# A spectral mixing and gated feed-forward kernel: the first two x tiles loaded in other pieces and from two queues

## The chip, the cores and the metric

The kernel runs on one core of one Trainium2 chip. The metric is the device time of one execution in microseconds (us). A core has a matrix engine (PE; PEld is its weight load, which runs beside the matmuls), a vector engine (DVE), a scalar engine (ACT), a general engine (POOL) and a sync engine (SP). Data moves between the main memory (DRAM) and the on-chip memory through 16 DMA engines. A transfer is issued by an instruction on some engine's queue: here nearly all by SP, 36 by ACT, and in later parts of the program some by POOL. SPq and ACTq in the profile are those issuing instructions.

## The reference

With x of 2048 rows and 512 columns, the reference normalizes each row, mixes it by two Fourier matrices and multiplies the result with a gate that comes from a two-layer network:

```
xn = _layernorm(x, axis=-1)
a = jnp.einsum("bsd,ed->bse", xn, dft_hid_re)
b = jnp.einsum("bsd,ed->bse", xn, dft_hid_im)
s = jnp.einsum("ts,bse->bte", dft_seq_re, a) - jnp.einsum("ts,bse->bte", dft_seq_im, b)
h = jnp.einsum("bsd,df->bsf", xn, w1) + b1
h = where(h > 0, h, 0) ** 2
g = _silu(jnp.einsum("bsf,fd->bsd", h, w2) + b2)
return x + s * g
```

The sequence matrices are 2048 x 2048, the hidden ones 512 x 512, w1 is 512 x 1792 and w2 1792 x 512. All are float32.

## The kernel before

Each float32 operand of a product is split into a high part, rounded by ACT (`split_hi`, line 134), and the rest, made by DVE (`split_lo`, line 137), and a product is three passes: high by high, high by low, low by high. The sequence product comes first. Its columns are cut into eight chunks of 256 (c = 0 to 7), and the sum over the 2048 rows into eight steps (j = 0 to 7). Step j takes the x tile j, 256 rows of x in two groups of 128 (h = 0 and 1: rows 128 j and 1024 + 128 j), one row on each of the 128 partitions, so that a tile has 128 x 2 x 512 numbers (512 KB), and the tile `u` of the sequence matrices for chunk c and step j (512 KB as well). Chunks 0 and 1 are plain products (`one_product`, line 377); chunks 2 to 7 use seven products in place of eight (`mm`, line 362). The hidden transform and the first layer (line 755) and the second layer (line 861) follow, and the output rows are finished beside the last.

The program is written in the order in which each engine runs it; no scheduler reorders it. In chunk 0 the normalization of the x tiles runs beside the products. For each step j:

- the transfers of x tile j (`load_x`, line 200) and of `u` (`load_c`, line 273), on SP's queue
- mean and variance of each row. For tile 0 DVE does it for both groups (`ln_stats`, lines 204 and 205). From tile 1 on, DVE does it for h = 0 and ACT for h = 1: the mean (`ln_mean`, line 209) and the variance (`ln_var`, lines 214 and 144)
- the root on ACT (`ln_root`, line 221), the reciprocal and a correction step on DVE (`ln_rstd`, lines 226 to 230)
- the normalized tile `xn` on DVE (`ln_xn`, line 237), its high part `xc` on ACT (line 134), its low part on DVE (line 137), and the split of `u` into `g` in the same two lines
- 24 matmuls of 512 columns (line 377), which read `xc` and `g`

Ahead of these, PE runs 14 matmuls on zeros (line 483), which no result uses. Each engine runs its instructions in order. On DVE the instructions of the first steps stand like this: statistics of tile 0, group 0; statistics of tile 0, group 1; the reciprocal for group 0; its `xn`; the low part of `g`; the reciprocal for group 1; its `xn`; a low part; statistics of tile 1, group 0; two low parts; the reciprocal for tile 1. On ACT: a table load and a root of a constant (line 465), the two roots of tile 0, the high parts of `g` and `xc` in turn, then mean and variance of tile 1, group 1, and the root of tile 1.

The transfers stand ahead of all this, and all go to SP's queue:

```
    nc.scalar.activation(stats[:, 1, 0, 0:1], eps, AF.Sqrt)
    for hs in (one, two):
        load_x(0, hs)
    for hs in (one, two):
        load_c(0, 0, hs)
    for j in range(1, 3):
        load_x(j)
        load_c(0, j)
    load_x(3)
```

`one` is the group h = 0 and `two` the group h = 1, or the first and the second half of a `u` tile. So tile 0 comes in two transfers of 256 KB, `u` of step 0 in two of 256 KB, and what follows in transfers of 512 KB.

Of the kernel before, what the change touches and what calls it, by code (L numbers as in the profile page):

```python
# [13 lines left out]
P = 128  # L14
# [114 lines left out]
def fnet_gated_kernel(ctx, tc, x, xt, ct, wd, w1, w2, b1, b2, out):  # L129
    nc = tc.nc  # L130
# [24 lines left out]
    rows = dram.tile([2 * NS, P], F32, name="rows")  # L155
# [12 lines left out]
    def buf(tag, shape, name, dtype=F32):  # L168
        return pool.tile(shape, dtype, tag=tag, bufs=3 if tag == "u" else 1, name=name)
# [24 lines left out]
    xr, xn32 = {}, {}  # L194

    def load_x(j, hs=slice(0, 2)):

        if j not in xr:
            xr[j] = buf(X_ROOM[j], [P, 2, D], f"x{j}")
        nc.sync.dma_start(xr[j][:, hs], x.rearrange("(h j p) d -> j p h d", h=2, p=P)[j][:, hs])  # L200

    def ln_stats(j, h=0):
        bn = small[:, j % 3, 6 * h:6 * h + 6]
# [65 lines left out]
    def load_c(c, j, hs=slice(0, 2)):  # L269
        if (c, j) not in raw:  # L270
            raw[c, j] = buf("u", [P, 8, CW], f"u{c}_{j}")
        q = slice(2 * hs.start, 2 * hs.stop)
        nc.sync.dma_start(raw[c, j][:, q], ct[c, j, :, q])
# [107 lines left out]
    one, two = slice(0, 1), slice(1, 2)  # L381
# [80 lines left out]
    makers["y"] = y_early  # L462
    makers["p"] = load_wd

    nc.scalar.activation(stats[:, 1, 0, 0:1], eps, AF.Sqrt)
    for hs in (one, two):
        load_x(0, hs)
    for hs in (one, two):
        load_c(0, 0, hs)
    for j in range(1, 3):  # L470
        load_x(j)
        load_c(0, j)
    load_x(3)

    warm = bank("b30", "warm")
# [120 lines left out]
    for n, s in enumerate(steps):  # L596
        c, j = s
# [445 lines left out]
    for n in range(NTC * NP):  # L1043
        c, p = divmod(n, NP)
# [110 lines left out]
def _launch(arrays, out_shape):  # L1155
    import numpy as np
    import concourse.bacc as bacc
    from concourse.bass_utils import run_bass_kernel_spmd

    nc = bacc.Bacc("TRN2", target_bir_lowering=False, num_devices=1, dynamic_dma_scratch_size=1024)  # L1160
    feed, args = {}, []
    for name, v in arrays.items():
        v = np.ascontiguousarray(v)
        feed[f"in_{name}"] = v
        args.append(nc.dram_tensor(f"in_{name}", v.shape, mybir.dt.from_np(v.dtype), kind="ExternalInput").ap())
    args.append(nc.dram_tensor("out_0", out_shape, F32, kind="ExternalOutput").ap())
    with tile.TileContext(nc, schedule_with_timeline_sim=True) as tc:
        fnet_gated_kernel(tc, *args)
    r = run_bass_kernel_spmd(nc, [feed], core_ids=[0])
    return r.results[0]["out_0"]  # L1170
# [25 lines left out]
```

## Time and profile before

| what | value |
|---|---|
| three runs | 673.10, 673.64, 673.92 us; median 673.64 |
| the profiled execution's own time | 673.52 us |
| its span, from the first instruction to the last | 671.7 us |
| granted clock of PE | 0.999 |
| busy: PE, DVE, ACT | 665.4, 597.3, 379.0 us |
| moved by DMA | 150.82 MB, 225 GB/s on average |

The profiled execution took 1.8 us more than its span, before the first instruction and after the last one. Times in the views count from the start of the span. In the view in order of time a row gives start, duration, engine, line, operation, what is written and read, how many instructions stand in the row, and in brackets how long the engine was idle before it and what ended that. A row of the chain of waits gives start, duration and what took it, followed back from the last instruction. A row of the stretches gives the stretch, its length, the busy time of PE, PEld, DVE, ACT and POOL with the number of their instructions, PE's granted clock, the share of the DMA engines and GB/s. A row on transfers gives what is moved, the engine that issues it, how many, KB of each, and us from issue to landing. q1 is SP's DMA queue and q10 ACT's; a row on a queue gives its packets, MB and its share of the 16 engines.

### The profile page before, as it was taken

To read this page: it belongs to the slowest core of one execution; us is meant where nothing else is said; L and a number is where in the kernel's file an instruction comes from. 1 tells how busy PE (TensorE), PEld (TensorE's weight loads), DVE (VectorE), ACT (ScalarE), POOL (GpSimd) and SP (SyncE) were. 2 spreads that over 40 slices of the span, in tenths; PEclk is the share of its full clock that TensorE was granted. 3 is DMA by queue.
4 is the path that set the end of the run, shared out by engine and by line. 5 is a ranking of instruction groups with operands and counts; after the bars stand their busy time and mean duration, and the time that the engine had idled before them with its cause. 6 is when DMAs were issued, how large, how long until landed. Compare 5 with 4: busy or idle time off the path is not lost.

```text
span 671.7 us, 13186 instructions
## 1 busy us (share of the span) xinstructions
PE 665.4 (99%) x5438; PEld 646.5 (96%) x5438; DVE 597.3 (89%) x833; ACT 379.0 (56%) x524; POOL 8.8 (1%) x11
## 2 busy tenths in 40 slices
PE   8999999999999999999999999999999999999997
PEld 5888889999999999999999999999999999999997
DVE  7997888999999999799899989877887889999997
ACT  6856554534445454444365547788778765454451
POOL 0000000000000000000000000000000000101011
PEclk9999999999999999999999999999999999999999
DMA  8635768646556774759688557665755866777765
GB/s 306 212 100 218 255 232 277 214 148 213 211 168 225 248 286 162 261 164 344 200 296 279 194 188 297 222 246 209 267 183 198 326 241 212 181 230 176 232 205 156
DMA packets 51739, 150.82 MB, mean 225 GB/s; under 512 B 4960, under 2 KB 19552, under 8 KB 50272
## 3 DMA queue, kind: packets, MB, share of 16 engines
q1 hardware_dynamic: 43568, 129.28, 57.1%
q10 hardware_dynamic: 6208, 18.88, 7.1%
q0 software_dynamic: 1904, 1.84, 1.9%
q8 instruction: 42, 0.69, 0.4%
q14 instruction: 17, 0.14, 0.1%
HBM read 101.98 MB, written 47.99 MB: 223 GB/s over the span
## 4 chain that ended last, share of the span: by engine, by line
PE 94%; DVE 2%; DMA 2%; ACT 1%; issue 0%; SPq 0%; DVEq 0%; ACTq 0%
PE m L362 32%; PE m_o L861 15%; PE r_B L755 13%; PE r_A L755 9%; PE pq_b L377 8%; PE r_C L755 4%; PE r_D L755 4%; PE m_last L861 4%; PE pq_ba L377 2%; PE pq_bc L377 1%; PE pq_bb L377 1%; DMA u<-in_ct 1%; DMA x<-in_x 1%; DVE g L137 1%; DVE z L1111 0%; DVE z L911 0%
## 5 line engine op out<-in xcount | busy, mean ns | idle before, releaser
L362 PEld LDWEIGHTS m<-g,xc 128*128 128x128 f32 x2016 | 229.1, 188 | 0.3 <-DVE g L137 0.2
L362 PE MATMUL m<-g,xc 128*128 128x256 f32 x2016 | 229.3, 276 | 0.1
L134 ACT ACTIVATE g<-u 128x1792 fp32r<-128x1792 f32 (+2 forms) x65 | 99.0, 1523 | 132.1 <-PE m L362 92.6
L137 DVE TENSOR_TENSOR g<-u,g 128x1792 fp32r<-128x1792 f32 (+2 forms) x65 | 116.8, 1797 | 19.3 <-ACT g L134 18.8
L861 PE MATMUL m_o<-w,g 128*128 128x256 f32 x882 | 100.5, 276 | 0.0
L861 PEld LDWEIGHTS m_o<-w,g 128*128 128x128 f32 x882 | 100.3, 188 | 0.0
L134 ACT ACTIVATE g<-hr 128x1792 fp32r<-128x1792 f32 (+2 forms) x31 | 48.2, 1566 | 39.9 <-DVE hr L296 17.7
L755 PE MATMUL r_B<-xT,w 128*128 128x256 f32 x504 | 66.5, 276 | 0.0
L377 PE MATMUL pq_b<-g,xc 128*128 128x512 f32 x240 | 65.2, 391 | 1.0 <-ACT xc L134 1.0
L755 PEld LDWEIGHTS r_B<-xT,w 128*128 128x128 f32 x504 | 61.4, 188 | 0.0
L137 DVE TENSOR_TENSOR g<-hr,g 128x1792 fp32r<-128x1792 f32 (+2 forms) x31 | 56.7, 1838 | 3.0 <-ACT g L134 2.8
L377 PEld LDWEIGHTS pq_b<-g,xc 128*128 128x128 f32 x240 | 44.8, 188 | 11.3 <-ACT xc L134 1.9
L755 PE MATMUL r_A<-xT,w 128*128 128x256 f32 x336 | 42.8, 276 | 0.0
L755 PEld LDWEIGHTS r_A<-xT,w 128*128 128x128 f32 x336 | 40.2, 188 | 0.0
L755 PE MATMUL r_B<-wdp,yg 128*128 128x256 f32 x288 | 35.9, 277 | 0.0
L284 DVE TENSOR_TENSOR u<-u 128x512 f32<-128x512 f32 x48 | 32.9, 685 | 3.0 <-DMA u<-in_ct 3.0
L755 PEld LDWEIGHTS r_B<-wdp,yg 128*128 128x128 f32 x288 | 34.1, 188 | 0.1
L861 PE MATMUL m_last<-w,g 128*128 128x256 f32 x294 | 33.5, 276 | 0.0
L861 PEld LDWEIGHTS m_last<-w,g 128*128 128x128 f32 x294 | 33.4, 188 | 0.0
L137 DVE TENSOR_TENSOR yg<-yraw,yg 128x1792 fp32r<-128x1792 f32 x13 | 26.2, 2018 | 0.7 <-ACT yg L134 0.7
L134 ACT ACTIVATE yg<-yraw 128x1792 fp32r<-128x1792 f32 x13 | 22.2, 1707 | 5.4 <-DVE yraw L293 4.4
L755 PE MATMUL r_D<-xT,w 128*128 128x256 f32 x168 | 23.6, 276 | 0.0
(187 smaller groups left out, 876.8 us busy)
## 6 DMA issues: line engine op xcount, KB each, us to landing
u<-in_ct SPq DMA_DIRECT2D x63, 512.0 KB, 3.9
hd<-h ACTq DMA_DIRECT2D x28, 512.0 KB, 4.0
hr<-hd SPq DMA_DIRECT2D x28, 512.0 KB, 3.7
wdp<-wdd SPq DMA_DIRECT2D x8, 896.0 KB, 7.2
yraw<-pqd SPq DMA_DIRECT2D x13, 512.0 KB, 6.0
pqd<-c SPq DMA_DIRECT2D x6, 1024.0 KB, 6.2
w<-w1d SPq DMA_DIRECT2D x6, 896.0 KB, 8.2
y<-y ACTq DMA_DIRECT2D x8, 512.0 KB, 5.5
```

The costliest lines, as they stand in the source:

```text
L134: nc.scalar.activation(hi, src, AF.Copy)
L137: nc.vector.tensor_tensor(lo, src, hi.bitcast(F32), op=ALU.subtract)
L284: nc.vector.tensor_tensor(t[:, 0:2], r[:, 0:1].to_broadcast([P, 2, 256]), r[:, 1:3], op=ALU.add)
L362: nc.tensor.matmul(ps[:, d], w[:, a_, d * P:(d + 1) * P], halves(mv(b_)), start=first and d == 0 and (a_, b_) == (HI, HI), stop=last and ( ...
L377: nc.tensor.matmul(accs[c][k], w, part[c, j][:, b_, 2 * h:2 * h + 2], start=j == 0 and h == 0 and (a_, b_) == (HI, HI), stop=j == NJ - 1 a ...
L755: nc.tensor.matmul(self.region(REGION[k]), w, mv, start=i == 0 and k in (1, 7), stop=i == len(ops) - 1, skip_group_check=True)
L861: nc.tensor.matmul(m[:, i * 256:(i + 1) * 256], ready[n][:, a_, H_SLOT[a], i * P:(i + 1) * P], W2[p][:, b_, b], start=p == 0 and i == 0 an ...
```

## The change

```diff
-        nc.sync.dma_start(xr[j][:, hs], x.rearrange("(h j p) d -> j p h d", h=2, p=P)[j][:, hs])
+        src = x.rearrange("(h j p) d -> j p h d", h=2, p=P)[j]
+        if j == 0 and hs == one:
+            for q, rows in ((nc.sync, slice(0, P // 2)), (nc.scalar, slice(P // 2, P))):
+                q.dma_start(xr[j][rows, hs], src[rows, hs])
+        elif j == 0:
+            nc.scalar.dma_start(xr[j][:, hs], src[:, hs])
+        else:
+            nc.sync.dma_start(xr[j][:, hs], src[:, hs])
...
+    for hs in (one, two):
+        load_x(0, hs)
     nc.scalar.activation(stats[:, 1, 0, 0:1], eps, AF.Sqrt)
     for hs in (one, two):
-        load_x(0, hs)
-    for hs in (one, two):
         load_c(0, 0, hs)
-    for j in range(1, 3):
-        load_x(j)
-        load_c(0, j)
+    for hs in (two, one):
+        load_x(1, hs)
+    load_c(0, 1)
+    load_x(2)
+    load_c(0, 2)
     load_x(3)
```

Group 0 of tile 0 is loaded by two transfers of 64 partitions (128 KB each), the first from SP's queue and the second from ACT's. Group 1 of tile 0 follows whole on ACT's queue. Both ACT transfers stand ahead of ACT's table load. Tile 1 comes in two transfers of 256 KB on SP's queue, group 1 first. The number of transfers goes from 9 to 11 over these first lines; the bytes stay the same. The instructions of PE and DVE keep their number and order.

These are the first rows of SP's queue before. x_135, x_141, x_145 and x_149 are the x tiles 0 to 3, and u_0, u_1 and u_2 the `u` tiles of steps 0 to 2; x2 stands for two such instructions.

```order
L200 DMA x_135<-in_x 128x512 x2
L273 DMA u_0_138<-in_ct 128x512 x2
L200 DMA x_141<-in_x 128x2x512
L273 DMA u_1_143<-in_ct 128x1024
L200 DMA x_145<-in_x 128x2x512
L273 DMA u_2_147<-in_ct 128x1024
L200 DMA x_149<-in_x 128x2x512
```

And the first rows of SP's queue now, where x_134, x_142, x_147 and x_151 are the x tiles 0 to 3:

```order
L203 DMA x_134<-in_x 64x512
L280 DMA u_0_139<-in_ct 128x512 x2
L207 DMA x_142<-in_x 128x512 x2
L280 DMA u_1_145<-in_ct 128x1024
L207 DMA x_147<-in_x 128x2x512
L280 DMA u_2_149<-in_ct 128x1024
L207 DMA x_151<-in_x 128x2x512
```

One transfer is gone from ahead of the two `u` transfers of step 0, and tile 1 has two places where it had one, so that what follows it has as many transfers ahead of it on SP as before.

These are the first rows of ACT before:

```order
L465 ACT_TABLE_LOAD
L465 ACTIVATE stats<-eps 128x1
L221 ACTIVATE small<-stats,eps 128x1 x2
L134 ACTIVATE g_0_176<-u_0_138 128x512
L134 ACTIVATE xc_121<-xn_0_182 128x2x256
```

And now:

```order
L203 DMA x_134<-in_x 64x512
L205 DMA x_134<-in_x 128x512
L474 ACT_TABLE_LOAD
L474 ACTIVATE stats<-eps 128x1
L228 ACTIVATE small<-stats,eps 128x1 x2
L134 ACTIVATE g_0_178<-u_0_139 128x512
L134 ACTIVATE xc_121<-xn_0_184 128x2x256
```

Two transfers, the other half of tile 0's first group and all of its second group, are now ahead of the table load.

## The prediction

> **What bounds the kernel now.** I read the page first, then the stretches, PE in order of time, the chain of waits, and at last DVE, ACT and the transfers of the first 14 us.
>
> The page's busy times, and four stretches:
>
> ```profile
> PE 665.4 (99%) x5438; PEld 646.5 (96%) x5438; DVE 597.3 (89%) x833; ACT 379.0 (56%) x524; POOL 8.8 (1%) x11
> ...
> 7.13:13.12 5.99, 5.79 (x25) 4.42 (x25) 5.51 (x16) 4.55 (x11) 0.00 (x0) 1.00 1.02 390
> 13.12:285.00 271.88, 271.88 (x2036) 257.53 (x2037) 243.69 (x335) 140.52 (x165) 0.00 (x0) 1.00 0.62 216
> 285.00:287.00 2.00, 1.95 (x16) 1.75 (x16) 2.00 (x4) 1.85 (x2) 0.00 (x0) 1.00 0.10 16
> 287.00:667.00 380.00, 380.00 (x3348) 379.87 (x3347) 339.94 (x462) 228.31 (x341) 8.65 (x7) 1.00 0.69 229
> ```
>
> PE is busy without a gap from 13.12 to 667 us, except for 0.05 us near 286. So the end moves with the moment at which PE starts step 1 of chunk 0 (13.12), one for one; the change touches only transfers ahead of that. PE's rows up to there:
>
> ```profile
> 1.22 5.10 PE L483 MATMUL warm<-idle 128*128 128x512 bf16 x14 [1.22 <-DVE idle L479]
> 7.13 0.73 PE L377 MATMUL pq_b<-g,xc 128*128 128x512 f32 x2 [0.81 <-ACT xc L134]
> ...
> 12.53 0.39 PE L377 MATMUL pq_bc<-g,xc 128*128 128x512 f32 x1
> 13.12 0.73 PE L377 MATMUL pq_b<-g,xc 128*128 128x512 f32 x2 [0.20 <-ACT xc L134]
> ```
>
> Matmuls of step 0 start 0.23 us apart, so step 1 could have started at 12.53 + 0.23 = 12.76. It starts 0.36 later, because `xc` of tile 1 is late. The chain of waits says why, by its own account:
>
> ```profile
> 0.74 0.39 SPq L200
> ...
> 1.19 0.42 SPq L200
> ...
> 1.65 0.42 SPq L273
> ...
> 2.12 0.43 SPq L273
> 2.59 5.90 DMA x<-in_x
> 8.52 0.72 ACT junk L209 x2
> ...
> 10.73 0.31 ACT small L221
> 11.85 0.56 DVE xn L237
> ...
> 13.12 0.73 PE pq_b L377 x2
> ```
>
> The reader is to see four issues on SP, then tile 1 under way for 5.90 us until 8.49, then ACT's mean, variance and root, DVE's `xn`, PE. It looks as if all that tile 1 gains were gained at the end. DVE's rows say otherwise:
>
> ```profile
> 3.43 0.69 DVE L204 BATCH_NORM_STATS2 small<-x 128x6 f32<-128x512 f32 x1 [1.72 <-DMA x<-in_x]
> 4.23 0.18 DVE L205 BATCH_NORM_AGGREGATE stats<-small 128x2 f32<-128x6 f32 x1
> 4.33 0.66 DVE L204 BATCH_NORM_STATS2 small<-x 128x6 f32<-128x512 f32 x1
> ...
> 5.12 0.13 DVE L226 RECIPROCAL small<-small 128x1 f32<-128x1 f32 x1
> ...
> 8.77 0.69 DVE L204 BATCH_NORM_STATS2 small<-x 128x6 f32<-128x512 f32 x1
> ...
> 10.18 0.68 DVE L137 TENSOR_TENSOR xc<-xn,xc 128x512 fp32r<-128x512 f32 x1
> 11.06 0.17 DVE L226 RECIPROCAL small<-small 128x2 f32<-128x2 f32 x1 [0.20 <-ACT small L221]
> ```
>
> From 3.43, when group 0 of tile 0 has landed, DVE is occupied up to tile 1's reciprocal at 11.06, and waits there for only 0.20 us. There are thus two chains of nearly equal length: tile 1 through ACT, and tile 0 through DVE, 0.20 us shorter. Tile 0's chain also sets PE's first start (7.13).
>
> **The change part by part.** The rows for the transfers, in the order of issue on SP (0.74, 1.19, 1.65, 2.12, 2.59), with the time to landing last, and ACT's rows:
>
> ```profile
> x<-in_x SPq DMA_DIRECT2D x1, 256.0 KB, 2.7
> x<-in_x SPq DMA_DIRECT2D x1, 256.0 KB, 2.9
> u<-in_ct SPq DMA_DIRECT2D x1, 256.0 KB, 3.9
> u<-in_ct SPq DMA_DIRECT2D x1, 256.0 KB, 4.6
> x<-in_x SPq DMA_DIRECT2D x1, 512.0 KB, 5.9
> ```
>
> ```profile
> 0.73 1.28 ACT L465 ACT_TABLE_LOAD   x1 [0.73 <-PEq L1160]
> ...
> 4.45 0.29 ACT L221 ACTIVATE small<-stats,eps 128x1 f32<-128x1 f32 x1 [2.22 <-DVE stats L205]
> ...
> 6.98 0.61 ACT L134 ACTIVATE g<-u 128x512 fp32r<-128x512 f32 x1
> 8.52 0.60 ACT L209 ACTIVATE junk<-x 128x512 f32<-128x512 f32 x1 [0.92 <-DMA x<-in_x]
> ```
>
> So the landings are 3.4 and 4.1 (tile 0), 5.5 and 6.7 (`u` of step 0) and 8.5 (tile 1).
>
> *Two issues ahead of ACT's table load.* At 0.4 us each, as SP's, they put the load at about 1.6 and its end at 2.9. ACT's next work is at 4.45, after 2.22 us of idleness. Cost 0; the cover is gone only if the load took over 1 us longer.
>
> *Tile 1 in two, group 1 first.* SP has one issue less ahead, so group 1 is issued at about 2.12 and has 1.25 MB up to its end in place of 1.5. Between the landings at 6.7 and 8.5, half the way is 7.6; that is when ACT comes to line 209 anyway (8.52 - 0.92 = 7.60). ACT's 0.92 us of waiting goes, but DVE, late next, needs 11.06 - 0.20 for its own work: the term is -0.20. Group 0 of tile 1 is issued at 2.6 as before, lands by 8.5, and DVE asks for it at 8.77. Cost 0, with 0.27 of cover. What follows tile 1 is issued no later than before.
>
> *Group 0 of tile 0 from two queues.* Landing 3.4 is bounded by no change from above, and from below by half the 0.70 us that lie between the two landings of tile 0, thus 3.05. It would start DVE up to 0.35 earlier. The Trainium skill, "DMA: Bandwidth & Descriptors", section "Rules for kernel authors", says not to bother with two transfers to disjoint partition halves, because both use the same 16 engines. By that rule the landing stays at 3.4; the trace before has no such pair, so it can't say. I take 3.4, since the same 256 KB have to pass, and keep 3.05 as an end; it counts only if group 1 keeps pace.
>
> *Group 1 of tile 0 on ACT's queue.* This is the term that decides. DVE does the statistics of group 1 (4.33) ahead of the reciprocal for group 0 (5.12), and all the rest is behind them. Group 1 landed at 4.1, so it had 0.2 us to spare. It is issued at about 1.19 as before, but until now nothing else was issued then: the first half of `u` came 0.46 later, behind it. Now SP issues `u` at the same moment, and both share the engines. Two rows on sharing, for 413 to 416 us, where both queues had work:
>
> ```profile
> q1 hardware_dynamic: 124, 0.80, 68.2%
> q10 hardware_dynamic: 95, 0.39, 31.5%
> ```
>
> Packets go about one for one. Then group 1 ends when about three times 256 KB have passed in place of two. At the 0.70 us that 256 KB took between tile 0's landings this is 4.1 + 0.70 = 4.8; at the pace of `u`, whose first half landed third at 5.5, it is 5.5 (upper end). The lower end is 4.1 - 0.35 = 3.75, if both queues fill the engines sooner and group 1 stays ahead. I take 4.8, the pace of the same rows of x. DVE's second statistics then start at 4.83 in place of 4.33: +0.50, for PE's first start (7.6) and for all that DVE does up to tile 1.
>
> **Sum:** +0.50 - 0.20 = +0.3 us: step 1 starts at 13.4, after a first start at 7.6, so PE's wait between the steps shrinks to 0.16. From there PE is full as before. Ends: landing at 5.5 gives 5.53 - 4.33 - 0.20 = +1.0; 3.75 with 3.05 gives -0.35 - 0.20 = -0.55. Against the profiled execution's own 673.52 the sum is 673.8, and against the median, 0.12 above that, 673.9.
>
> **The rivals.** 0.2% of this time, 1.35 us, is about what a measurement of this kernel can tell from no change; three runs lay between 673.1 and 673.9.
>
> *A: group 1 keeps its place.* ACT's issue is at the engines before SP's `u`, and lands at 4.1 or sooner. Then only -0.20 is left, with up to 0.35 more: 673.1 to 673.4. For it: ACT starts at 0.73, SP at 0.74, and the second issues come out even. Against it: packets of two queues alternate.
>
> *B: slower, ACT's transfer waits behind SP's.* The rows for a transfer of ACT in the middle of the kernel, and for SP's packets between 409 and 412.9:
>
> ```profile
> 408.99 0.34 ACTq L845 DMA_DIRECT2D hd<-h  x1
> ...
> hd<-h ACTq DMA_DIRECT2D x1, 512.0 KB, 9.5
> ...
> q1 hardware_dynamic: 276, 1.33, 95.9%
> ```
>
> The whole of 409 to 412.9 belongs to q1: ACT's transfer moved nothing for 4 us, and landed after 9.5. If group 1 waits like that behind both halves of `u`, it lands no sooner than 6.7: 6.73 - 4.33 - 0.20 = +2.2, 675.8; behind tile 1 too, at 8.5, +4.0, 677.6. It decides from a landing of 5.9 on (5.88 - 4.33 - 0.20 = 1.35). Against it: at 409 SP's queue had megabytes waiting, while at 1.19 each queue has one transfer under way. The page "DMA: Bandwidth & Descriptors" of the Trainium skill, section "Queues, rings and completion order", has each engine go round the queues packet by packet; by that rule B can't happen and 4.8 stands. The rows at 413 agree, those at 409 don't, so B keeps a chance.
>
> *C: a remainder.* Another placement of transfers, or a first transfer on ACT's queue that starts slowly, shifts a later wait such as the one near 286. No row prices it.
>
> **How the numbers follow.** Forecast (-0.1 to +1.0): 0.53. A: 0.25. B: 0.14. C: 0.08, half to each side. Within 0.2% lie nearly all of the forecast and of A: 0.50 + 0.23 = 0.73. Slower are B, 0.03 of the forecast and half of C: 0.20. Faster is the rest, 0.07. The forecast's own range is 673.5 to 674.7. The range takes A's -0.55 and the forecast's +1.0 with 0.4 us for the scatter of the runs, and the nearest part of B: 672.7 to 675.4. It leaves out most of B and C.
>
> **What would show it.** Right: DVE's second statistics start near 4.8 and wait there for a DMA; PE's first real matmul is near 7.6 and step 1 near 13.4; ACT has no wait ahead of the mean of tile 1; the 0.20 us ahead of the reciprocal near 11 is gone; after that PE has no new gap. Wrong: the second statistics at 4.3 or sooner (A), or after 5.9 (B); or a wait of DVE for group 0 of tile 1 near 9, whose 0.27 of cover I count as enough; or a changed gap of PE after 14 us (C).

## The result and the profile after

The changed kernel takes 674.46 us (median of 21 runs, 673.43 to 676.82), the kernel before 673.22 (21 runs, 672.75 to 674.33). The ratio is 1.0018, 95% interval 1.0012 to 1.0024: 1.2 us slower, inside the 0.2% that the prediction counts as no change, but clear of zero. The new times also spread over 3.4 us, the old ones over 1.6. The profiled execution took 674.05 us, with a span of 672.3.

PE in order of time, changed kernel:

```profile
1.22 5.90 PE L492 MATMUL warm<-idle 128*128 128x512 bf16 x14 [1.22 <-DVE idle L488]
7.85 0.73 PE L384 MATMUL pq_b<-g,xc 128*128 128x512 f32 x2 [0.72 <-ACT xc L134]
...
13.19 0.39 PE L384 MATMUL pq_bc<-g,xc 128*128 128x512 f32 x1
13.55 0.72 PE L384 MATMUL pq_b<-g,xc 128*128 128x512 f32 x2
```

The first real matmul is at 7.85 (before 7.13), step 1 at 13.55 (13.12), its wait shorter (13.55 - 13.19 - 0.23 = 0.13 in place of 0.36). Three later stretches of the same kernel:

```profile
13.12:285.00 271.88, 271.88 (x2035) 257.14 (x2034) 243.75 (x336) 140.71 (x166) 0.00 (x0) 1.00 0.62 217
285.00:287.00 2.00, 1.86 (x16) 1.66 (x15) 2.00 (x3) 1.79 (x3) 0.00 (x0) 1.00 0.00 0
287.00:667.00 380.00, 380.00 (x3350) 379.87 (x3350) 340.12 (x463) 228.83 (x341) 8.65 (x7) 1.00 0.69 229
```

PE has no gap there but 0.14 us near 286 (before: 0.05). So of the 0.53 us by which this profiled execution is longer than the one before, 0.43 lie ahead of 13.55. Small differences between single profiled executions can't be read further than that: from 285 to 287 us both hold 16 matmuls, where the profile of e1 below holds 20, and over the kernels of the next table the time that follows the start of step 1 lies between 659.64 us (e3, e6) and 661.01 us (e7). DVE, changed kernel:

```profile
4.14 0.69 DVE L211 BATCH_NORM_STATS2 small<-x 128x6 f32<-128x512 f32 x1 [2.44 <-DMA x<-in_x]
...
5.04 0.66 DVE L211 BATCH_NORM_STATS2 small<-x 128x6 f32<-128x512 f32 x1
...
10.90 0.68 DVE L137 TENSOR_TENSOR xc<-xn,xc 128x512 fp32r<-128x512 f32 x1
11.50 0.16 DVE L233 RECIPROCAL small<-small 128x2 f32<-128x2 f32 x1
```

The first statistics start at 4.14 in place of 3.43, 0.71 late: it is group 0 of tile 0 that DVE waits for. The second statistics follow at once, so group 1 is not the one that is late. The wait of 0.20 ahead of tile 1's reciprocal is gone: 0.71 - 0.20 = 0.51, of which 0.43 arrives at step 1. The issues of the two queues and the landing of ACT's half, of SP's half and of group 1, changed kernel:

```profile
0.74 0.57 ACTq L203 DMA_DIRECT2D x<-in_x  x1
1.34 0.60 ACTq L205 DMA_DIRECT2D x<-in_x  x1
...
0.74 0.60 SPq L203 DMA_DIRECT2D x<-in_x  x1
1.40 1.28 SPq L280 DMA_DIRECT2D u<-in_ct  x2
```

```profile
x<-in_x ACTq DMA_DIRECT2D x1, 128.0 KB, 2.7
x<-in_x SPq DMA_DIRECT2D x1, 128.0 KB, 3.3
...
x<-in_x ACTq DMA_DIRECT2D x1, 256.0 KB, 3.5
```

Each half takes 0.57 to 0.60 us to issue, where a whole group took 0.39. ACT's half lands at 3.45, hardly later than the whole group did (3.40); SP's half, issued at the same moment, at 4.04. Packets of the two queues from 2.0 to 2.6 us, and from 2.6 to 2.95:

```profile
q10 hardware_dynamic: 53, 0.11, 66.9%
...
q1 hardware_dynamic: 50, 0.10, 78.3%
q10 hardware_dynamic: 27, 0.02, 19.1%
```

Nothing of SP's half moves until 2.6, when ACT's is nearly through. The two are served one after the other.

### The profile page after: what moved, and what is told of

Same layout as the page of the kernel before. It is cut to its first block, busy times and chain, and to the rows that moved or that the text cites. A ratio compares the mean times of both kernels' runs of the same rounds, so it can differ in the third digit from the quotient of the medians.

```text
span 672.3 us, 13188 instructions
## 1 busy us (share of the span) xinstructions
PE 665.8 (99%) x5438; PEld 646.8 (96%) x5438; DVE 597.2 (89%) x833; ACT 379.1 (56%) x524; POOL 8.8 (1%) x11
## 4 chain that ended last, share of the span: by engine, by line
PE 95%; DVE 2%; DMA 2%; ACT 1%; issue 0%; DVEq 0%; ACTq 0%
PE m L369 32%; PE m_o L870 15%; PE r_B L764 13%; PE r_A L764 9%; PE pq_b L384 8%; PE r_C L764 4%; PE r_D L764 4%; PE m_last L870 4%; PE pq_ba L384 2%; PE pq_bc L384 2%; PE pq_bb L384 2%; DMA u<-in_ct 1%; DVE g L137 1%; DMA x<-in_x 0%; DVE z L1120 0%; DVE z L920 0%
```

## The experiments

Each kernel was compared with the kernel before on the same chip. Where a time is "against" another, both are medians of that comparison.

| kernel | group 0 of tile 0 | group 1 | tile 1 | median, before | ratio (95%) | step 1 in the profile |
|---|---|---|---|---|---|---|
| changed | 2 x 64 partitions, SP and ACT | ACT | two pieces | 674.46, 673.22 | 1.0018 (1.0012 to 1.0024) | 13.55 |
| e1 | whole, SP | SP | two pieces | 673.08, 673.17 | 0.9997 (0.9988 to 1.0006) | 12.98 |
| e2 | 2 x 64, SP and ACT | SP | whole | 674.07, 673.17 | 1.0013 (1.0004 to 1.0021) | 14.40 |
| e3 | whole, SP | ACT | whole | 673.36, 673.17 | 1.0002 (0.9993 to 1.0011) | 13.46 |
| e4 | whole, SP; b1 on ACT | SP | whole | 673.11, 673.17 | 0.9997 (0.9989 to 1.0006) | 13.40 |
| e5 | 2 x 64, both SP | SP | whole | 674.02, 672.99 | 1.0013 (1.0004 to 1.0022) | 14.01 |
| e6 | whole, SP | ACT | two pieces | 673.09, 672.99 | 1.0001 (0.9993 to 1.0010) | 13.30 |
| e7, changed again | as changed | ACT | two pieces | 674.20, 672.99 | 1.0020 (1.0010 to 1.0030) | 16.28 |
| e8 | 2 x 256 columns, SP and ACT | ACT | two pieces | 674.08, 672.99 | 1.0013 (1.0004 to 1.0022) | 13.72 |
| e9 | 2 x 256 columns, SP and ACT | SP | two pieces | 673.86, 673.11 | 1.0010 (1.0000 to 1.0019) | 13.00 |

The kernel before has 13.12. After the first comparison the suspicion was theory T, that two queues which issue at the same moment hold each other up, against rival U, the prediction's own account.

### e1: tile 1 alone

```diff
-    for j in range(1, 3):
-        load_x(j)
-        load_c(0, j)
+    for hs in (two, one):
+        load_x(1, hs)
+    load_c(0, 1)
+    load_x(2)
+    load_c(0, 2)
     load_x(3)
```

> The kernel before with one part of the change alone: tile 1 in two transfers on SP's queue, group 1 first; tile 0 whole from SP as before. The prediction's term for this part is -0.20 us, because DVE's own work up to tile 1's reciprocal is only 0.20 us shorter than the chain through ACT: the wait of 0.20 us near 11 goes, ACT has no wait ahead of the mean of tile 1, and step 1 starts near 12.9 in place of 13.12; the time -0.2 us (ratio 0.9997). The rival, read from the chain of waits alone, has all of ACT's 0.92 us come back: step 1 then starts at 12.76, -0.36 us. If instead the added issue on SP harms what follows it, step 1 or a later step starts later than before.

DVE and PE of e1:

```profile
10.34 0.68 DVE L137 TENSOR_TENSOR xc<-xn,xc 128x512 fp32r<-128x512 f32 x1
10.94 0.15 DVE L226 RECIPROCAL small<-small 128x2 f32<-128x2 f32 x1
```

```profile
12.60 0.39 PE L377 MATMUL pq_bc<-g,xc 128*128 128x512 f32 x1
12.98 0.73 PE L377 MATMUL pq_b<-g,xc 128*128 128x512 f32 x2
```

DVE's wait is gone and step 1 is 0.14 earlier. So the chain through tile 1, which held the whole stretch by the chain of waits, was worth 0.14 us and not the 0.36 of PE's wait. In the time (-0.1 us) this can't be told from nothing.

### e2: the halves alone

```diff
+        src = x.rearrange("(h j p) d -> j p h d", h=2, p=P)[j]
+        if j == 0 and hs == one:
+            for q, rows in ((nc.sync, slice(0, P // 2)), (nc.scalar, slice(P // 2, P))):
+                q.dma_start(xr[j][rows, hs], src[rows, hs])
+        else:
+            nc.sync.dma_start(xr[j][:, hs], src[:, hs])
```

> The kernel before with the other part alone and only its first half: group 0 of tile 0 in two halves by partitions, one from SP's queue and one from ACT's; group 1 of tile 0 stays on SP's queue and tile 1 whole. Theory T (transfers of two queues issued at the same moment are served one whole after the other and lengthen each other's issue): ACT's half lands near 3.4, SP's half near 4.0, DVE's first statistics start near 4.1 in place of 3.43, step 1 near 13.6, +0.4 to +0.6 us. Rival U (the engines share by packets, as predicted, and only group 1 beside u is late): both halves land at 3.4, the first statistics start at 3.4, step 1 at 13.1, 0.

DVE of e2:

```profile
3.98 0.69 DVE L209 BATCH_NORM_STATS2 small<-x 128x6 f32<-128x512 f32 x1 [2.27 <-DMA x<-in_x]
...
5.23 0.69 DVE L209 BATCH_NORM_STATS2 small<-x 128x6 f32<-128x512 f32 x1 [0.27 <-DMA x<-in_x]
```

Group 0 is late as theory T had it, group 1 too, and tile 1, which is whole here and issued at 3.21 in place of 2.59, lands at 9.8. Step 1 comes at 14.40, later than in the changed kernel. Rival U falls for this part, and theory T had the landings right but not the size: it put step 1 near 13.6 and the time at +0.4 to +0.6 us. The time is +0.9 us, so the halves alone bring most of the changed kernel's cost.

### e3: group 1 alone on ACT's queue

```diff
+        q = nc.scalar if j == 0 and hs == two else nc.sync
+        q.dma_start(xr[j][:, hs], src[:, hs])
```

> The kernel before with only group 1 of tile 0 moved to ACT's queue; group 0 whole on SP's queue, tile 1 whole. Theory T: one of the two transfers is served whole ahead of the other. If ACT's is first, as it was in the changed kernel, group 1 lands near 3.4 to 3.5 and group 0 only near 4.2; DVE starts near 4.2, step 1 near 13.7 to 13.9, +0.5 to +0.8 us. If SP's is first, group 0 lands at 3.4 and the time is 0 to +0.2. Rival U: both groups share and land near 4.1, in packets that alternate from the first one on.

The issue on SP, and the packets from 2 to 3 us, e3:

```profile
0.74 0.39 SPq L202 DMA_DIRECT2D x<-in_x  x1
...
q1 hardware_dynamic: 79, 0.16, 50.8%
q10 hardware_dynamic: 77, 0.16, 45.9%
```

With 128 partitions the issue takes 0.39 us on SP and 0.40 on ACT, and in this stretch the packets go one for one. Both groups land near 4.1, DVE starts at 4.05, step 1 is at 13.46. Here rival U was right and theory T fell: of two queues that issue at once, neither is held back until the other is through. One thing stands against a simple account of the cost: group 0 lands at 4.03 here, as late as in the changed kernel, and step 1 comes at 13.46 against 13.55, yet the median rises by only 0.2 us and not by 1.2.

### e4: a small transfer on ACT's queue

```diff
+    nc.scalar.dma_start(b1s, b1)
     nc.scalar.activation(stats[:, 1, 0, 0:1], eps, AF.Sqrt)
...
-            nc.sync.dma_start(b1s, b1)
```

> The kernel before with all of tile 0 on SP's queue as before; only the transfer of b1 (7 KB, until now issued by SP after step 2) is issued by ACT at the start, ahead of its table load. It moves 1% of what tile 0 moves, so rival U expects no change: group 0 lands at 3.4. Theory T: what costs is a second queue issuing at the same moment, not the bytes: SP's first issue takes 0.5 to 0.6 us in place of 0.39, its first packet comes 0.3 to 0.5 us later, group 0 lands at 3.7 to 3.9, and the time is +0.3 to +0.5 us.

SP's first issue took 0.39, group 0 landed at 3.47 and DVE started at 3.49. The time did not move. Theory T fell for the second time. What was left as the cause of the slow issue and landing was the transfer of 64 partitions itself. That is theory H, tested next.

### e5: the halves, both on SP

```diff
+            for rows in (slice(0, P // 2), slice(P // 2, P)):
+                nc.sync.dma_start(xr[j][rows, hs], src[rows, hs])
```

> The kernel before with group 0 of tile 0 in two transfers of 64 partitions, both from SP's queue; nothing on ACT's queue. Theory H (a transfer of 64 partitions is itself slow to issue and to start, on whichever queue): SP's two issues take about 0.6 us each in place of one of 0.39, the first packet comes near 2.1 in place of 1.76, group 0 lands near 4.0, DVE starts near 4.1, everything behind on SP is 0.8 us later, tile 1 lands near 9.3 and step 1 starts near 13.9: +0.8 us. Rival Q (the harm needs the second queue): issues of 0.39, group 0 lands at 3.4 to 3.6, step 1 at 13.1 to 13.5, 0 to +0.4 us.

SP's issues and DVE of e5:

```profile
0.74 1.23 SPq L203 DMA_DIRECT2D x<-in_x  x2
2.02 0.58 SPq L205 DMA_DIRECT2D x<-in_x  x1
```

```profile
4.05 0.69 DVE L209 BATCH_NORM_STATS2 small<-x 128x6 f32<-128x512 f32 x1 [2.34 <-DMA x<-in_x]
```

Two halves on one queue cost 1.23 us of issue in place of 0.39, and the transfer behind them 0.58. Group 0 lands at 3.95, step 1 is at 14.01 (+0.89), the time +1.0. Without any second queue the cost is near that of the changed kernel. Theory H holds here for the issue, the landing and step 1, and rival Q falls. Part of step 1's delay is here that everything behind on SP is issued later: tile 1 lands at 9.39 in place of 8.49.

### e6: the changed kernel with group 0 whole

```diff
-        if j == 0 and hs == one:
-            for q, rows in ((nc.sync, slice(0, P // 2)), (nc.scalar, slice(P // 2, P))):
-                q.dma_start(xr[j][rows, hs], src[rows, hs])
-        elif j == 0:
+        if j == 0 and hs == two:
             nc.scalar.dma_start(xr[j][:, hs], src[:, hs])
```

> The changed kernel with one part undone: group 0 of tile 0 again in one transfer of 128 partitions from SP's queue; group 1 stays on ACT's queue, tile 1 in two transfers. Theory H: issues are back at 0.4 us, both groups share the engines and land near 4.1, DVE starts near 4.1, tile 1 is early enough for all; step 1 starts near 13.4, +0.1 to +0.3 us against the kernel before, and 0.9 to 1.1 us below the changed kernel's 674.46. Rival Q: the second queue is what costs, so it stays near the changed kernel, 674.2 to 674.6.

The time is 0.1 us above the kernel before, against 1.2 for the changed kernel: undoing the halves undoes the loss. Issues are back at 0.38 to 0.42, step 1 is at 13.30. The profiles show only part of that difference: group 0 lands at 3.87 here against 4.04 in the changed kernel, and step 1 is 0.25 earlier, while the medians lie about 1.1 us apart.

### e7: the changed kernel again

> The changed kernel once more, for another look at its first 14 us. Its times lay between 673.4 and 676.8, while the profiled execution took 674.05 and its step 1 starts only 0.43 later than before. If the spread comes from the start, the landings of tile 0 and tile 1 or the order in which the pieces are served differ from the first look (group 1 behind the first half of u, or tile 1 near 9 to 10), and step 1 starts elsewhere, 13.5 to 15. If it comes from later, step 1 is at 13.5 again and the time differs by what follows it, by more than the 0.7 us by which the kernels so far differ there.

The profiled execution took 677.29 us, at the upper end of the spread. DVE and PE of e7:

```profile
4.02 0.69 DVE L211 BATCH_NORM_STATS2 small<-x 128x6 f32<-128x512 f32 x1 [2.31 <-DMA x<-in_x]
...
6.24 0.69 DVE L211 BATCH_NORM_STATS2 small<-x 128x6 f32<-128x512 f32 x1 [1.24 <-DMA x<-in_x]
```

```profile
9.08 0.73 PE L384 MATMUL pq_b<-g,xc 128*128 128x512 f32 x2 [1.91 <-ACT xc L134]
...
11.31 0.63 PE L384 MATMUL pq_bc<-g,xc 128*128 128x512 f32 x1
11.74 1.05 PE L384 MATMUL pq_b<-g,xc 128*128 128x512 f32 x2
...
16.28 0.62 PE L384 MATMUL pq_b<-g,xc 128*128 128x512 f32 x2
```

Group 0 is late as in the first profile. Group 1, on ACT's queue beside u, landed at 6.22 in place of 4.83, so DVE waited a second time, and PE idled 1.91 us. Packets of the two queues of e7 from 4.0 to 6.3 us:

```profile
q1 hardware_dynamic: 394, 0.72, 92.8%
q10 hardware_dynamic: 8, 0.01, 1.6%
```

From 2 to 4 us ACT's queue had moved 216 packets. So nearly all of group 1 was through by 4.0, and a last few packets made it late, not an even sharing with u. Then step 0 took 16.28 - 9.08 = 7.20 us, 1.5 more than in the first profile. Stretches of e7 show why:

```profile
6.80:10.20 3.40, 1.50 (x7) 0.94 (x6) 3.08 (x14) 2.58 (x6) 0.00 (x0) 1.00 0.99 386
10.20:13.60 3.40, 3.40 (x10) 2.62 (x9) 3.22 (x10) 2.79 (x6) 0.00 (x0) 0.50 0.79 284
13.60:16.28 2.68, 2.68 (x13) 2.19 (x12) 2.68 (x5) 2.16 (x5) 0.00 (x0) 1.00 0.91 346
```

After a stretch of 3.4 us in which PE was busy for 1.50, the granted clock fell to 0.50 for the next 3.4 us, and matmuls started 0.43 us apart in place of 0.23. So this execution's time does come from the start: group 1's landing, and the clock on top of it. It is not shown that the other executions of the spread are like it. The mean granted clock of each execution is on record: it is 0.997 in this one, in one more of e7's twelve (675.97 us) and in two of the 23 of the kernel before that were measured with e9 (674.97 and 675.42 us), but not below 0.998 in any of the 21 executions of the first comparison. So a fall of this kind is found in a few long executions; it does not make the median.

### e8: the halves by columns

```diff
-            for q, rows in ((nc.sync, slice(0, P // 2)), (nc.scalar, slice(P // 2, P))):
-                q.dma_start(xr[j][rows, hs], src[rows, hs])
+            for q, rows in ((nc.sync, slice(0, D // 2)), (nc.scalar, slice(D // 2, D))):
+                q.dma_start(xr[j][:, hs, rows], src[:, hs, rows])
```

> The changed kernel with group 0 of tile 0 halved the other way: 128 partitions and 256 columns on each of the two queues (128 KB each, pieces of 1 KB) in place of 64 partitions and 512 columns. The number of transfers, queues and bytes is that of the changed kernel. Theory H: the issues take 0.4 us again, both halves start at 1.8 and share the engines, group 0 lands at 3.4 to 3.6, group 1 near 4.8, step 1 near 13.3 to 13.5, 673.2 to 673.7. Rival Q, or any cost of two transfers for one tile: as the changed kernel, 674.2 to 674.6.

DVE of e8:

```profile
3.48 0.69 DVE L211 BATCH_NORM_STATS2 small<-x 128x6 f32<-128x512 f32 x1 [1.78 <-DMA x<-in_x]
...
5.17 0.69 DVE L211 BATCH_NORM_STATS2 small<-x 128x6 f32<-128x512 f32 x1 [0.71 <-DMA x<-in_x]
```

Theory H was right on issue and landing: with 128 partitions the issues take 0.38 and 0.41 and group 0 lands at 3.46. Yet the time stayed at 674.08, not the 673.2 to 673.7 expected, and nearer to the 674.2 to 674.6 of the rival (any cost of two transfers for one tile). In the profile group 1, issued beside u at 1.18, now lands at 5.15 and DVE waits for it. This is the prediction's term by itself, and here it is 5.17 - 4.33 = 0.84 us. Step 1 is 0.60 late, of 1.1 us in the median; the rest this profile does not show.

### e9: the halves by columns, group 1 back on SP

```diff
-            nc.scalar.dma_start(xr[j][:, hs], src[:, hs])
+            nc.sync.dma_start(xr[j][:, hs], src[:, hs])
```

> The kernel with group 0 of tile 0 halved by columns on the two queues, with group 1 of tile 0 back on SP's queue, ahead of u; tile 1 in two transfers. In the variant with group 1 on ACT's queue it was issued at the same moment as u, shared the engines with it packet by packet, landed at 5.15 and held DVE for 0.71 us. Theory S (that sharing is the price of group 1's move): with group 1 ahead of u on one queue it lands near 4.1 again, DVE's second statistics do not wait, step 1 starts at 12.8 to 13.1 in place of 13.72, and the time is 672.7 to 673.2, 0.9 to 1.3 us below. Rival: what costs there is the halving itself, also by columns; then step 1 stays near 13.7 and the time near 674.0.

The profiled execution went as theory S had it: group 1 at 4.24, no wait for it, step 1 at 13.00, 673.04 us. The median did not: 673.86, with executions from 672.81 to 675.52. The profiled one was the second fastest of twelve. In the median the rival was nearer, the halving itself, which put the time near 674.0. So group 1 beside u delays DVE in the profile of e8, but halves by columns cost something else as well in the median, and no profile shows what.

### e10: 64 partitions in another place

```diff
+    xr[1] = buf(X_ROOM[1], [P, 2, D], "x1")
+    for part64 in (slice(0, P // 2), slice(P // 2, P)):
+        nc.sync.dma_start(xr[1][part64], x.rearrange("(h j p) d -> j p h d", h=2, p=P)[1][part64])
```

> The kernel before with tile 1 in two transfers of 64 partitions (both groups in each), all else as before. Theory H (64 partitions are slow to issue wherever they stand): the two issues and the one behind them take 0.55 to 0.6 us in place of 0.43, tile 1 lands 0.3 to 0.8 later than 8.49, at 8.8 to 9.3, and the pieces land one after the other with a gap of the engines between them. Rival: only the first transfers of a program are slow; then the issues take 0.43 and tile 1 lands at 8.5.

SP's issues of e10:

```profile
1.65 0.90 SPq L273 DMA_DIRECT2D u<-in_ct  x2
2.59 1.40 SPq L472 DMA_DIRECT2D x<-in_x  x2
4.04 0.59 SPq L273 DMA_DIRECT2D u<-in_ct  x1
```

The two halves take 1.40 us to issue (0.75 and 0.61 each) and the transfer behind them 0.59 in place of 0.47. It is 64 partitions, not the first place. The time (one execution, 675.46) can't be laid to the edit: the first half of u, issued ahead of it, landed at 7.4 in place of 5.5, PE idled 1.92 us, and the clock fell as in e7:

```profile
5.90:9.30 3.40, 1.48 (x7) 0.92 (x6) 1.58 (x5) 1.67 (x3) 0.00 (x0) 1.00 1.03 259
9.30:12.70 3.40, 3.40 (x10) 2.63 (x9) 3.33 (x7) 2.06 (x6) 0.00 (x0) 0.50 1.03 388
```

### e11: the changed kernel, a third profile

> The changed kernel, one more look. Both looks so far had issues of 0.56 to 0.60 us, the first packet at 2.1, group 0 at 3.9 to 4.0; they differ in group 1 (4.83 and 6.22), because it shares the engines with u, and one engine can be far behind. Expected: the first three again, group 1 between 4.8 and 6.2, and step 1 later than 13.12 by what group 1 is behind 4.3, less 0.2 to 0.4.

One execution, 673.51 us. Issues 0.56 to 0.60, first packet at 2.1, group 0 at 3.99, DVE at 4.09: as in both profiles before. Group 1 landed at 4.54, a little below the range expected, and delayed nothing, since DVE came to it at 4.99. Step 1 is at 13.49, by group 0's delay alone.

### e12: four matmuls on zeros fewer

```diff
-WARM = 8, 6
+WARM = 8, 2
```

> The kernel before with 2 in place of 6 of the second kind of matmuls on zeros, so that PE is idle for some 1.9 us ahead of its first real matmul in place of 0.81, as in the slow look of the changed kernel (1.91 us), while every transfer lands as before. Theory C (that idleness itself lets the granted clock fall to half for one stretch of 3.41 us, and costs 1.7 us): part or all of the executions take 1.5 to 2 us more, 674.5 to 675.2, and their step 0 shows a clock of 0.5 and matmuls 0.43 us apart. Rival: the fall had another cause; then the time stays at 673.0 to 673.5.

The median is 673.98, against 673.11 (1.0017, 1.0005 to 1.0029). Six of twelve executions took 672.87 to 673.55, as before the edit, and six 674.41 to 676.71. The matmuls on zeros of the profiled one (676.71), and its step 0, up to its twelfth matmul and after it:

```profile
1.22 4.45 PE L483 MATMUL warm<-idle 128*128 128x512 bf16 x10 [1.22 <-DVE idle L479]
```

```profile
8.22:13.24 5.02, 5.02 (x12) 3.97 (x13) 4.74 (x15) 3.87 (x10) 0.00 (x0) 1.00 0.99 368
13.24:16.17 2.93, 2.93 (x14) 2.36 (x13) 2.90 (x6) 2.78 (x7) 0.00 (x0) 1.00 0.88 324
```

About 12 matmuls in 5.02 us, then 14 in 2.93: half speed, then full. The clock column does not show it here, the matmuls do. But this is not the fall that theory C meant. The 10 matmuls on zeros took 4.45 us and started 0.43 us apart, so PE ran at half speed before it went idle. In the kernel before, 14 of them take 5.10 us, less than the 5.6 us that 13 steps of 0.43 would take, so these reach full speed on the way. In this execution full speed came only within step 0: the clock had not fallen, it had not yet risen. The edit takes four matmuls away as well as adding idleness, so it is no test of idleness alone, and theory C stays open. What is shown is that with four matmuls on zeros fewer, half of the executions take 674.41 us or more. This execution is not pure either, since group 1 also landed late in it (5.36), though it was issued from SP as in the kernel before; the idleness was 2.55 us and not 1.9.

## Why the prediction was right and where it was wrong

- *Total.* +0.3 us was forecast, +1.24 was measured. The range held it, the side is right, and it is still within 0.2%; the size is off by a factor of four. That side and range were met is in part luck: the +0.3 came from group 1, late by 0.50, with group 0 at no change, while in two of three profiles of the changed kernel group 0 was the late one and DVE did not wait for group 1. (The shares that the prediction adds up for slower, 0.14, 0.03 and 0.04, give 0.21 and not 0.20.)
- *Group 0 of tile 0 from two queues, "I take 3.4".* This step of the prediction failed. It had no change as its upper end, on the ground that the same 256 KB have to pass. In three profiles group 0 landed at 4.04, 3.92 and 3.99, because each half takes 0.56 to 0.60 us to issue and the second is served behind the first. I had no row for a transfer of 64 partitions and bounded it only by its bytes. In the table, four kernels with a whole group 0 have ratios of 0.9997 to 1.0002, the changed kernel and four others with halves 1.0010 to 1.0020. So it is shown that halving group 0 costs the time. It is not shown that the late landing is the path: in e3 and e6 group 0 landed at 4.03 and 3.87 and the medians rose by 0.2 and 0.1 us, and with halves by columns it landed at 3.46 (e8) and 3.58 (e9) and they rose by 1.1 and 0.75. The rule that the prediction quoted from the Trainium skill, "DMA: Bandwidth & Descriptors", section "Rules for kernel authors", says that the halves serialize, and the packets of the changed kernel agree (53 to 0). It also has the packets of two queues interleave, which these two halves did not do, and it speaks of no gain, where the runs show a loss of 0.6 us at the landing.
- *Group 1 on ACT's queue, +0.50 from a landing at 4.8.* The landing was 4.83 in the first profile, and a late group 1 beside u holds DVE by itself in e8 (5.15, +0.84). But in the first and third profile it did not decide, since DVE itself came 0.6 later; and in e7 it came at 6.22, beyond my upper end of 5.5, because of a last few packets. With group 0 whole, group 1 is issued at 0.73 beside group 0, and the move costs 0.1 to 0.2 us (e3, e6), which is not clear of zero.
- *Tile 1 in two, -0.20.* Right: the wait of 0.20 and ACT's 0.92 are gone in the changed kernel, and e1 gives 0.14 at step 1. Reading DVE's rows beside the chain of waits is what kept this term small.
- *ACT's table load, 0.* Right: it ran from 1.97 to 3.25, and ACT's next work came at 5.16.
- *Step 1 near 13.4, first matmul near 7.6.* 13.55 and 7.85 in the first profile, 13.49 and 7.79 in the third: near the forecast, but by group 0's delay and not by group 1's. These executions took 674.05 and 673.51; the median lies above them. They explain about 0.4 of the 1.24 us, and what fills the rest is not shown. A fall of the clock as in e7 is found in too few executions for it; a clock that rises late, as in e12's profile, leaves the recorded mean at 1.00, so whether it plays a part is open. I had read PE's idleness ahead of step 0 as a delay that passes one for one; it cost more where it was 1.91 and 1.92 us (e7, e10), and no fall of the clock followed 1.30 to 1.38 us (e2, e3, e5, e6).
- *Rivals.* A (group 1 keeps its place) was seen in no profile. B (ACT's transfer waits behind SP's) was not seen either: e7's landing of 6.22 lies past B's 5.9, but ACT's queue moved from 2 us on, and only its last 8 packets came after 4.0. C, a later wait, gave nothing between the two profiles: the gap near 286 went from 0.05 to 0.14 us.

What stays open is by what path halving group 0 costs most of its 0.75 to 1.24 us in the median, above all by columns, where issues and landing of group 0 are hardly slower; and why one of the first transfers lands 1 to 2 us late in some executions (group 1 in e7 and e12, the first half of u in e10), with or without a second queue. No profile was taken of an execution of e9 near its median. The loss of e9 is the least certain, since its interval reaches 1. No version is shown to beat the kernel before: e1, the fastest, has an interval across 1.

## What to carry to other kernels

Price a transfer by its shape as well as its bytes: here every kernel that halved one of 256 KB lost 0.75 to 1.24 us in the median, while moving a whole one to a second queue cost 0.1 to 0.2, not clear of zero. Where a chain of waits passes through a transfer, look how near the next chain is before you count the transfer's whole wait as gain; here 0.14 of 0.36 us came back. Ahead of the first matmuls, idleness of PE can be paid twice, once as delay and once in clock (e7, e10). And where the executions of one kernel spread over 3 us, one profile does not explain the median: compare the profiled time with it, and look for a kernel that shows the same delay without the cost, as e3 does here.

## What the runs showed of the hardware that was not expected

- A transfer of 64 partitions takes 0.56 to 0.75 us to issue and, among the first five of a queue, one of 128 partitions 0.38 to 0.47, on SP and ACT alike; a transfer issued right behind one of 64 partitions is slowed too (0.58 to 0.60, and 0.80 for the first half of u in the changed kernel). The first packet comes at 2.1 us in place of 1.76 where the program starts with one.
- Two transfers of 128 partitions on two queues share packet by packet (79 to 77 from 2 to 3 us in e3); two of 64 partitions on two queues did not (53 to 0 from 2.0 to 2.6 us in the changed kernel).
- The landing of a transfer can hang on a last few packets: in e7, 216 packets of ACT's queue moved from 2 to 4 us, and the last 8 came between 4.0 and 6.3.
- After 3.4 us in which PE was busy for 1.50 (e7) or 1.48 (e10), the clock was 0.50 for 3.4 us. The Trainium skill, "TensorE: Matmul & The Clock Gate", section "Part 1: The HAM clock gate", gives a window of about 3.4 us that runs freely and lets the clock fall after an idle window. The length agrees with these rows; that a window need not be idle throughout is what they add.
